# A state-space scan followed by a low-rank mixer: the list that orders every engine's work rewritten, the state's guard put on GpSimd, one step of the squares taken one word later

## The chip, the cores and the metric

The kernel runs on one core of a Trainium2 chip. Its five engines are TensorE (PE; PEld is its loading of weights), VectorE (DVE), ScalarE (ACT), GpSimd (POOL) and SyncE (SP), whose queue issues the DMAs. The metric is the time of one execution on the device, in microseconds (us); the median of several runs is compared.

## The reference

Two blocks follow each other. The first is a chunked scan with a state, the second mixes along the sequence by a product of rank 32 and then along the channels by a two-layer network.

```python
# x (4,8,768,32), a (4,8,768), B and C (4,8,768,16), fp32; chunks of 32
for c in range(nc):
    cum = np.cumsum(la, axis=-1)                # la: log a of this chunk
    L = np.exp(cum[:, :, :, None] - cum[:, :, None, :]) * causal
    M = np.einsum('bhin,bhjn->bhij', Cc, Bc) * L
    y_intra = np.einsum('bhij,bhjd->bhid', M, xc)
    y_inter = np.einsum('bhin,bhnd->bhid', Cc, state) * np.exp(cum)[:, :, :, None]
    y[:, :, sl] = y_intra + y_inter
    state = decay_full[:, :, None, None] * state + np.sum(Bx, axis=2)
# y as x (4, 768, 256); U (768,32), V (32,768), w_ch1 (256,1024), w_ch2 (1024,256)
u = x + (x.transpose(0, 2, 1) @ U @ V).transpose(0, 2, 1)
out = u + np.maximum(u @ w_ch1, 0.0) @ w_ch2
```

U, V, w_ch1 and w_ch2 are 64-bit floats in memory.

## The kernel before

There are four batches. The scan of a batch is cut along the sequence into three blocks of two 128-row tiles; a block is numbered k, twelve in all. The mixer of a batch works on three blocks j of 256 rows.

All work is written down in one list, the string of PLANS[1]. The function follow (L1070) takes its words one after the other and calls the step that each names; nothing is reordered afterwards, so the order of the words sets the order of each engine's queue, of SP's too. A word of the scan is a letter and a block, counted from batch 1: P-3 to P-1 are batch 0, P0 to P2 batch 1, P6 to P8 batch 3. The letters that the text below speaks of are:

- B, X, w, L: loads, issued by SP (L202). The first DMA of such a word is held until the last VectorE instruction written before the word has ended.
- c: a piece of the conversion of 64-bit words to fp32 (L409, VectorE and ScalarE), R: the refinement of a converted weight into three parts, near and low on ScalarE, far and both on VectorE (L447; a word is one half of it). Each part of such a step is called by a word of its own.
- P, D: B and C times their decays, on VectorE (D of batch 0 on POOL); T: their transposes; g: the products C with B; m, M: the causal mask on VectorE.
- s, u: the new state, its products and its update on VectorE; the copy Sm masked for each half of the heads (L654 on POOL in batch 0, L658 on ScalarE afterwards).
- n, i, j: the products within a chunk (L746), and with the state (L721), which are written in two words in batch 0: i, and j, the crossed half. y: the copies of the result, yT (L761, L766, L768, ScalarE). t: yT turned back into rows, O the same in batch 0.

A word of the mixer carries the batch as what it lags behind: U1.j.i and f1.j.i are batch 0, f0 batch 1, f-1 batch 2, f-2 batch 3. p is the product with U and its copy pT (L815), x the product with V, a the addition of it on VectorE. Blocks 0 and 1 of batch 0 use plain products (U, d1.0, d1.1) with the converted weights; all others use three products in the fp32r format with a split operand (S): f takes the first two terms, near and low, and a scaling on ScalarE (L858), e the third and the Relu, h the far and joined parts on VectorE, d the second layer in pieces, one a word.

From block 6 on the transposes of P's result go another way (squared, L543): VectorE transposes 32 by 32 squares, SP sends them to memory and fetches them back, turned, into T, and ScalarE makes the masked copy Cm from T (L558). The second T word of a block is the fetch and Cm.

The guard of the state concerns the two halves that write the same rows of a bank. The products of word j may only start when those of word i have ended. For this the first product of j waits for an instruction of another engine that had to come later anyhow: a mask, an update, a copy or an addition that was recorded between them (follows, L661). Where there is none, a one-column copy called settled is put on VectorE (apart, L666), which waits for the earlier products.

## Time and profile before

| what | us |
| --- | --- |
| runs of the kernel | 213.56, 214.67, 217.28 |
| median | 214.67 |
| profiled execution, its span | 216.2 |

The profiled execution is the one that all rows below are from. Its span, 216.2 us, lies between the second and the third run; it runs from the first to the last instruction that the profiler saw. In the rows, L177 stands for nearly all of VectorE's instructions, since a helper records them there; they are told apart by the tiles that they write and read. In the part that names who waited, "A <- B" says that A waited until B had ended.

### The profile page before, as it was taken

Reading aid. Unit: us, or ns where it says so; the run is one execution under the profiler, and the core shown is the slowest. Engines: PE = TensorE matmul, PEld = TensorE weight load, DVE = VectorE, ACT = ScalarE, POOL = GpSimd, SP = SyncE. Lnnn points to the kernel's source line nnn. Section 1 sums busy time; section 2 is a strip of 40 time slices with the busy share of each in tenths; the row PEclk is TensorE's granted clock in tenths of the full one; section 3 lists DMA queues with packets and bytes.
Section 4 is the critical chain, followed back from the end, with each engine's and each line's share of the span. In section 5 each row is a group of like instructions: output and inputs, shape, how many; then the busy total and the mean of one; then the engine's idle time right before and its main releaser. Section 6 shows DMA issues by size and latency. Waiting matters only on the chain.

```text
span 216.2 us, 7556 instructions
## 1 busy us (share of the span) xinstructions
PE 205.8 (95%) x3214; PEld 183.6 (85%) x3214; DVE 173.4 (80%) x363; ACT 121.0 (56%) x279; POOL 6.3 (3%) x22
## 2 busy tenths in 40 slices
PE   7988987999999999999999999899999999999994
PEld 4766755787889997998999998589998999999993
DVE  4498869988999999999899986759966398759841
ACT  3454646659968857186488451668612675444310
POOL 4121000000000000000000000000000000000000
PEclk9999997999999999999999999999999999999999
DMA  6998677996553379447666846544600000323344
GB/s 89 123 117 197 76 186 170 218 247 149 77 71 52 65 195 124 110 60 102 92 103 108 190 91 150 80 74 100 137 12 0 0 5 0 52 38 64 48 97 97
DMA packets 120177, 21.43 MB, mean 99 GB/s; under 512 B 110096, under 2 KB 118352, under 8 KB 120144
## 3 DMA queue, kind: packets, MB, share of 16 engines
q1 hardware_dynamic: 120144, 20.95, 53.3%
q8 instruction: 25, 0.41, 0.9%
q14 instruction: 8, 0.07, 0.1%
HBM read 14.39 MB, written 6.55 MB: 97 GB/s over the span
## 4 chain that ended last, share of the span: by engine, by line
PE 62%; DVE 22%; SPq 5%; ACT 4%; issue 3%; DMA 2%; POOL 0%; DVEq 0%; POOLq 0%; ACTq 0%
PE x L853 28%; PE z L853 21%; DVE words L177 7%; SPq L203 5%; DVE S L177 3%; DMA words<-in_moe_w_ch_dram 2%; DVE yT L177 2%; DVE w L177 2%; DVE M L177 2%; DVE BC L177 1%; PE x L139 1%; PE w L626 1%; PE x L591 1%; DVE u L177 1%; PE z L746 1%
## 5 line engine op out<-in xcount | busy, mean ns | idle before, releaser
L177 DVE SCALAR_TENSOR_TENSOR words<-words 128x512 fp32r<-128x512 f32 (+6 forms) x60 | 39.3, 668 | 2.6 <-ACT words L429 0.5
L853 PE MATMUL x<-words,w 128*128 128x256 f32 x288 | 38.5, 281 | 0.1
L853 PEld LDWEIGHTS x<-words,w 128*128 128x128 f32 x288 | 35.3, 189 | 1.8 <-issue 1.2
L853 PE MATMUL x<-u,w 128*128 128x256 f32 x240 | 34.6, 283 | 0.0
L853 PE MATMUL z<-u,w 128*128 128x256 f32 x240 | 33.0, 279 | 0.0
L858 ACT ACTIVATE x<-x 128x512 f32<-128x512 f32 (+1 forms) x27 | 15.5, 577 | 29.6 <-PE x L853 27.5
L853 PEld LDWEIGHTS x<-u,w 128*128 128x128 f32 x240 | 30.5, 188 | 0.6 <-ACT yT L766 0.3
L853 PEld LDWEIGHTS z<-u,w 128*128 128x128 f32 x240 | 30.0, 188 | 0.1
L858 ACT ACTIVATE z<-z 128x512 f32<-128x512 f32 (+1 forms) x24 | 13.6, 572 | 12.7 <-PE z L853 12.7
L853 PE MATMUL z<-words,w 128*128 128x256 f32 x144 | 19.9, 282 | 0.0
L853 PEld LDWEIGHTS z<-words,w 128*128 128x128 f32 x144 | 18.1, 189 | 0.9 <-issue 0.9
L177 DVE SCALAR_TENSOR_TENSOR words<-x,words 128x512 fp32r<-128x512 f32 x20 | 13.7, 683 | 5.4 <-ACT words L893 5.4
L177 DVE SCALAR_TENSOR_TENSOR words<-z,words 128x512 fp32r<-128x512 f32 x20 | 13.6, 682 | 2.3 <-ACT words L893 2.2
L893 ACT ACTIVATE words<-x 128x512 fp32r<-128x512 f32 x20 | 12.0, 598 | 3.6 <-PE x L853 3.6
L591 PE MATMUL x<-Cm,T 32*64 32x128 f32 x192 | 12.1, 310 | 1.6 <-DVE yT L177 1.2
L177 DVE TENSOR_TENSOR yT<-x,yT 128x384 f32<-128x384 f32 (+1 forms) x15 | 9.2, 614 | 5.5 <-PE x L853 2.7
L177 DVE SCALAR_TENSOR_TENSOR S<-S,kept,w 128x64 f32<-128x64 f32 x40 | 11.2, 279 | 2.3 <-PE w L626 0.6
L893 ACT ACTIVATE words<-z 128x512 fp32r<-128x512 f32 x20 | 11.8, 598 | 1.9 <-PE x L853 1.3
L658 ACT ACTIVATE Sm<-S,slot 128x128 f32<-128x128 f32 (+1 forms) x18 | 6.0, 386 | 9.9 <-DVE S L177 9.9
L591 PEld LDWEIGHTS x<-Cm,T 32*64 32x64 f32 x192 | 7.5, 131 | 4.1 <-DVE yT L177 1.5
L177 DVE TENSOR_TENSOR BC<-bc,F 128x512 f32<-128x512 f32 (+2 forms) x18 | 8.8, 517 | 2.6 <-ACT F L379 1.3
L591 PE MATMUL z<-Cm,T 32*64 32x128 f32 x192 | 10.5, 311 | 0.0
(154 smaller groups left out, 368.5 us busy)
## 6 DMA issues: line engine op xcount, KB each, us to landing
words<-in_moe_w_ch_dram SPq DMA_DIRECT2D x7, 512.0 KB, 5.3
squares<-w1f SPq DMA_DIRECT2D x52, 64.0 KB, 1.9
x<-in_x_dram SPq DMA_DIRECT2D x24, 128.0 KB, 4.0
out_dram<-o SPq DMA_DIRECT2D x32, 64.0 KB, 2.2
bc<-in_B_dram SPq DMA_DIRECT2D x24, 64.0 KB, 3.5
bc<-in_C_dram SPq DMA_DIRECT2D x12, 128.0 KB, 3.8
T<-squares SPq DMA_DIRECT2D x6, 256.0 KB, 3.9
ytok<-squares SPq DMA_DIRECT2D x6, 256.0 KB, 3.1
```

The source lines that it names most:

```text
L139: nc.tensor.matmul(out=t[:, :m * w].rearrange("p (m i) -> p m i", i=w), lhsT=ident, rhs=ident[:, None, :w].to_broadcast([P, m, w]), start= ...
L177: self.last = call(*args, **kwargs)
L203: op = nc.sync.dma_start(**kwargs)
L591: nc.tensor.matmul(out=g[r][cols, c], lhsT=s["T"][rows, 0, c, cols], rhs=s["Cm"][rows, :, :, ts(2 * c + p, Q)].rearrange("r v t i -> r v i ...
L626: nc.tensor.matmul(out=s["A"][p][ts(r, Q), v], lhsT=s["bd"][half, v, 2 * r:2 * r + 2].rearrange("p h n -> p (h n)"), rhs=x_sb[k][half, v, ...
L658: nc.scalar.activation(s["Sm"][:, sl, v], s["S"][:, sl, ts(v, D)], AF.Copy, scale=slot[:, v, None])
L746: product = nc.tensor.matmul(out=y[n][p][ts(v, Q), c], lhsT=x_sb[k][half, c, h], rhs=s["M"][half, h // 2, c, h % 2], start=fresh(k, n, p, ...
L853: nc.tensor.matmul(out=t, lhsT=lhsT, rhs=rhs, start=start, stop=True, skip_group_check=True)
L858: nc.scalar.activation(t, t, AF.Copy, scale=1.0 + EPS)
L893: nc.scalar.activation(gs[j, i][0], t, AF.Relu, scale=NEAR)
```

## The change

The list of PLANS[1] is written anew: the same words in another order, and one more T word for each of the blocks T3 to T8. That word is for the squares: two more yields stand between the fetch and the masked copy, so that Cm is recorded with the third T word instead of the second. The guard is no longer looked for: every j word, three in all, gets a settled copy, now on GpSimd, which waits for the products before it and for which the first product of j waits. The other lines of the diff (ASIDE, FARPOOL) are switches that stay off, and a buffer's allocation at whichever half comes first. VectorE then has two copies less, GpSimd three more; the totals of all other instructions are equal.

```diff
@@ PLANS[1], the part up to the first long product @@
-        'i-3 g-2 u-2 j-3 y-3 F2 g-1 i-2 B3 B4 B5 w2 w3 X3 w4 X4 m-2 M-2 w5 c0 c0 m-1 B6 O-3.0 c0 M-1 '
-        'w6 E-1.1 n-2 s-1 u-1 c2 v0 w7 c1 c2 j-2 F3 i-1 y-2 j-1 n-1 c1 y-1 P0 D0 c1 T0 c2 t-2 O-1.3 '
-        'P2 X5 T0 X6 w8 P1 D2 p1.0.4 p1.4.6 c3 c3 x1 a1.0 a1.1 T1 T2 T2 T1 g0 U1.0.0 c3 c4 c4 U1.0.1 '
+        'u-2 n-3 g-2 m-2 i-3 w2 j-3 B3 w0 w1 y-3 M-2 B5 c0 c0 F2 g-1 c0 m-1 M-1 B4 w3 i-2 n-2 '
+        'E-1.1 s-1 u-1 w6 c3 O-3.0 X3 v0 P0 j-2 y-2 c2 F3 i-1 n-1 c1 c1 c1 X4 w4 P2 t-2 D0 w8 '
+        'j-1 w5 y-1 p1.0.4 c2 O-1.3 w7 X5 T0 c2 T2 p1.4.6 P1 D1 T0 B6 x1 a1.0 T2 L4 T1 c3 a1.1 '
+        'T1 g0 c3 U1.0.0 c7 c4 c4 U1.0.1 m0 U1.1.0 M0 c4 R2 R0 g1 m1 c7 s0 u0 U1.1.1 M1 c5 c5 s1 '
...
@@ squared @@
         fetch(s["T"].rearrange("p i c t -> p (i c) t"), d, sent)
+        yield
+        yield
         for i in range(2):
             nc.scalar.activation(s["Cm"][:, i], s["T"][:, 1], AF.Copy, scale=slot[:, i, None])
         yield
@@ update, mask, added, ytokening: their calls of follows go @@
-    def follows(op, turn):
-
-        if turn == behind["turn"]:
-            behind.setdefault("part", op)
-
-    def apart(copy):
-
-        behind["part"] = op = copy(out=settled, in_=slot[:, :1])
+    def apart():
+
+        op = nc.gpsimd.tensor_copy(out=settled, in_=slot[:, :1])
         for product in behind["first"]:
             tc.add_manual_dep(op.ins, product.ins.name, mybir.DependencyInfo(
                 mybir.DependencyClass.Sync, mybir.DependencyReason.DATA))
+        return op
@@ inter @@
-        if part and "part" not in behind:
-            apart(vector.tensor_copy)
-        after = behind.pop("part", None)
-        if part == 0:
-            after = None
-            behind["turn"] += 1
-        else:
+        after = None
+        if part:
+            after = apart()
             behind["first"] = []
```

What the rewritten list moves shows best in the queues. In the rows that follow, each gives the line, the operation, the tile written and the tiles read with their numbers in the program, and the shape.

The first place is the start, ahead of U1.0.0. SP's queue between U's words and the fourth load of w_ch1, before: words_325 is w0 and w1, bc_442, bc_446 and bc_450 are B3, B4 and B5 (three DMAs each, the C one shown), words_454 is w2.

```order
L203 DMA words_325<-in_moe_w_ch1_dram 128x2x256 x2
...
L203 DMA bc_442<-in_C_dram 128x8x32
...
L203 DMA bc_446<-in_C_dram 128x8x32
...
L203 DMA bc_450<-in_C_dram 128x8x32
...
L203 DMA words_454<-in_moe_w_ch1_dram 128x2x512
```

And now: words_402 is w2, bc_411 is B3, words_415 is w0 and w1, bc_422 is B5, bc_461 is B4.

```order
L207 DMA words_402<-in_moe_w_ch1_dram 128x2x512
...
L207 DMA bc_411<-in_C_dram 128x8x32
...
L207 DMA words_415<-in_moe_w_ch1_dram 128x2x256 x2
...
L207 DMA bc_422<-in_C_dram 128x8x32
...
L207 DMA bc_461<-in_C_dram 128x8x32
```

w2 has moved from the end of this set to its head, and B4 from the middle to the end.

VectorE's queue at the same place before, from P2 and P1 (BC) over D2 (bd) and the conversion c3 of w2 (words_706) to the four additions a1.0 and a1.1 (yT):

```order
L177 TENSOR_TENSOR BC_673<-bc_450,F_149 128x512
L177 TENSOR_TENSOR BC_688<-bc_446,F_149 128x512
L177 TENSOR_TENSOR bd_690<-bc_450,FD_150 128x256
L177 TENSOR_SCALAR words_706<-words_454 128x512 x2
L177 TENSOR_TENSOR yT_158<-x_712,yT_158 128x384
L177 TENSOR_TENSOR yT_158<-z_714,yT_158 128x384
L177 TENSOR_TENSOR yT_158<-x_713,yT_158 128x384
L177 TENSOR_TENSOR yT_158<-z_715,yT_158 128x384
```

And now, where BC_701 is P1 and bd_703 is D1:

```order
L181 TENSOR_TENSOR BC_701<-bc_461,F_149 128x512
L181 TENSOR_TENSOR bd_703<-bc_461,FD_150 128x256
L181 TENSOR_TENSOR yT_158<-x_714,yT_158 128x384
L181 TENSOR_TENSOR yT_158<-z_716,yT_158 128x384
L181 TENSOR_TENSOR yT_158<-x_715,yT_158 128x384
L181 TENSOR_TENSOR yT_158<-z_717,yT_158 128x384
L181 SCALAR_TENSOR_TENSOR words_533<-words_532,words_533 128x512
```

P2 stands far ahead now, the conversion of w2 has begun before this row of work and ends behind it, and P1 has come right before the additions.

GpSimd's queue in batch 0 before, the copies Sm of the state and the last D words:

```order
L488 TENSOR_TENSOR bd_289<-bc_91,FD_150 128x256
L654 TENSOR_TENSOR Sm_337<-S_336,slot_145 128x256
L654 TENSOR_TENSOR Sm_396<-S_395,slot_145 128x256
L488 TENSOR_TENSOR bd_268<-bc_95,FD_150 128x128
L654 TENSOR_TENSOR Sm_547<-S_546,slot_145 128x192
```

And now:

```order
L668 TENSOR_TENSOR Sm_288<-S_287,slot_145 128x256
L505 TENSOR_TENSOR bd_294<-bc_95,FD_150 128x128
L668 TENSOR_TENSOR Sm_333<-S_332,slot_145 128x256
L677 COPY settled_155<-slot_145 128x1
L505 TENSOR_TENSOR bd_294<-bc_95,FD_150 128x128
L668 TENSOR_TENSOR Sm_525<-S_524,slot_145 128x192
L677 COPY settled_155<-slot_145 128x1 x2
```

Three settled copies have come, the first behind the second Sm, the other two behind the third.

The second place is the middle, where VectorE refines the weights for the first fp32r products. Before, the last rows up to the refinement R1, whose two rows are those of words_1234 and the w12_79 behind it; the pair before it is R0:

```order
L177 SCALAR_TENSOR_TENSOR S_1172<-S_1172,kept_151,w_1093 128x64
L177 TENSOR_TENSOR words_1179<-w1f_80,w10_77 128x512
L177 SCALAR_TENSOR_TENSOR w12_79<-words_1179,w10_77 128x2x256
L177 TENSOR_TENSOR BC_1188<-bc_482,F_149 128x512
L177 TENSOR_TENSOR u1_1191<-yT_158,u0_1190 128x512
L177 SCALAR_TENSOR_TENSOR u2_1192<-u0_1190,u1_1191 128x512
L177 TENSOR_TENSOR words_1234<-w1f_80,w10_77 128x512
L177 SCALAR_TENSOR_TENSOR w12_79<-words_1234,w10_77 128x2x256
```

And now, where R1 is the pair of words_1240, and pairs that read o belong to the second layer's weights, R5:

```order
L181 TENSOR_TENSOR u1_1197<-yT_158,u0_1196 128x512
L181 SCALAR_TENSOR_TENSOR u2_1198<-u0_1196,u1_1197 128x512
L181 TENSOR_TENSOR words_1220<-w1f_80,w10_77 128x512
L181 SCALAR_TENSOR_TENSOR w12_79<-words_1220,w10_77 128x2x256
L181 TENSOR_TENSOR words_1224<-o_928,w20_81 128x512
L181 SCALAR_TENSOR_TENSOR w22_83<-words_1224,w20_81 128x512
L181 TENSOR_TENSOR words_1236<-w1f_80,w10_77 128x512
L181 SCALAR_TENSOR_TENSOR w12_79<-words_1236,w10_77 128x2x256
L181 TENSOR_TENSOR words_1240<-w1f_80,w10_77 128x512
L181 SCALAR_TENSOR_TENSOR w12_79<-words_1240,w10_77 128x2x256
```

R0, R5 and R3 now stand as three pairs ahead of R1; before, R0 alone did, and R2 and R5 came behind.

The third place is ScalarE's queue where batch 3's scan meets batch 2's mixer. Before, from the copies Sm over y6 (yT_2453) to the near part of batch 2's first block (u0):

```order
L658 ACTIVATE Sm_2399<-S_2398,slot_145 128x3x32 x2
L768 COPY yT_2453<-x_2405 128x2x64
L768 COPY yT_2453<-z_2407 128x2x64
L766 COPY yT_2453<-x_2406 64x2x64 x2
L766 COPY yT_2453<-z_2408 64x2x64 x2
L815 COPY pT_2461<-w_2462 128x128
L558 ACTIVATE Cm_2279<-T_2278,slot_145 128x256 x2
L847 ACTIVATE u0_2564<-yT_1758 128x512
```

And now:

```order
L672 ACTIVATE Sm_2382<-S_2381,slot_145 128x4x32 x2
L819 COPY pT_2453<-w_2454 128x128
L772 COPY yT_2480<-x_2417 128x2x64
L772 COPY yT_2480<-z_2419 128x2x64
L770 COPY yT_2480<-x_2418 64x2x64 x2
L770 COPY yT_2480<-z_2420 64x2x64 x2
L577 ACTIVATE Cm_2301<-T_2300,slot_145 128x256 x2
L850 ACTIVATE u0_2600<-yT_1722 128x512
```

The copy pT has moved from behind the copies of y6 to ahead of them.

More of the change, by code (lines that the diff above doesn't have):

```diff
@@ L17 @@
 PLAIN = 2
+ASIDE = 99
+FARPOOL = False
 SQUARED = 6
@@ L439, in to_fp32 @@
             w2f[n] = dst
+        if aside:
+            nc.gpsimd.tensor_tensor(out=dst, in0=wide(rest), in1=wide(power.bitcast(FP32)),
+                                    op=ALU.mult)
+            yield
+            return
         vector.scalar_tensor_tensor(
@@ L467 @@
     UU = const.tile([P, NC, 2, RK], FP32)
-    behind = {"turn": 0, "first": []}
+    behind = {"first": []}
     yT, ytok = {}, {}
@@ L737, in intra @@
         y = channels(k)
-        behind.pop("part", None)
-        behind["turn"] += 1
         for n in range(2):
@@ L789, in ytokening @@
             copy = nc.scalar.copy if b < 2 else vector.tensor_copy
-            behind.setdefault("part", copy(out=out, in_=t))
+            copy(out=out, in_=t)
         yield
@@ L824, in mixed @@
             hold["h"] = h
-            hold["turn"] = behind["turn"]
         def added(k):
@@ L830, in added @@
                 u = uT[:, n, ts(k, VS)]
-                follows(vector.tensor_tensor(
-                    out=u, in0=hold["h"][2 * n + k][:, :VS], in1=u, op=ALU.add), hold["turn"])
+                vector.tensor_tensor(
+                    out=u, in0=hold["h"][2 * n + k][:, :VS], in1=u, op=ALU.add)
         def block(j):
@@ L864, in plain @@
         def plain(j, i):
-            if i % 2 == 0:
+            if (j, i // 2) not in gT:
                 gT[j, i // 2] = words(FP32)
```

28 lines of the change are left out of this document (16 added, 12 removed), and 57 rows, old and new, of the table PLANS.

## The prediction

> **What bounds the kernel now.** I read the profile's page first (the busy times), then the busy time of each engine by stage, then, where an engine waits, its timeline.
>
> ```profile
> span 216.2 us, 7556 instructions
> PE 205.8 (95%) x3214; PEld 183.6 (85%) x3214; DVE 173.4 (80%) x363; ACT 121.0 (56%) x279; POOL 6.3 (3%) x22
> 17.00:36.00 19.00, 15.54 (x371) 11.45 (x372) 15.12 (x41) 11.57 (x29) 1.48 (x3) 0.97 0.75 149
> 36.00:66.00 30.00, 29.69 (x534) 24.30 (x533) 27.58 (x63) 21.70 (x51) 0.00 (x0) 0.96 0.74 154
> 66.00:98.00 32.00, 31.98 (x437) 28.74 (x438) 31.17 (x61) 21.32 (x45) 0.00 (x0) 1.00 0.56 103
> 98.00:132.00 34.00, 33.87 (x623) 32.16 (x613) 29.98 (x61) 20.06 (x52) 0.00 (x0) 1.00 0.65 114
> 132.00:145.00 13.00, 12.30 (x423) 9.59 (x412) 10.05 (x24) 7.21 (x24) 0.00 (x0) 1.00 0.50 95
> ```
>
> The five stage rows give from:to, length, then busy time of PE, PEld, DVE, ACT, POOL, then the granted clock, the DMA share and GB/s. From 36 us on TensorE is the bound: 29.69 of 30, 31.98 of 32, 33.87 of 34. The change reorders work and takes no matmul away, so all that a better order can win is PE's idle time: 3.46 us in 17 to 36 (19.00 - 15.54), about 0.5 in 36 to 132, 0.7 in 132 to 145. What a worse order can lose is not bounded so: VectorE stands at 31.17 of 32 between 66 and 98, so PE's rest there hangs on VectorE being in time. The start is another regime; there DMA and VectorE decide when the first long product (U1.0.0) may begin:
>
> ```profile
> 19.18 0.63 DVE L177 TENSOR_SCALAR words<-words 128x384 int32<-128x384 int32 x2 [0.87 <-DMA words<-in_moe_U_dram]
> 21.92 0.75 DVE L177 TENSOR_TENSOR M<-z,causal 128x256 int32<-128x256 int32 x2
> ...
> 30.10 1.29 DVE L177 TENSOR_TENSOR BC<-bc,F 128x512 f32<-128x512 f32 x2 [1.29 <-DMA bc<-in_B_dram]
> 31.31 0.42 DVE L177 TENSOR_TENSOR bd<-bc,FD 128x256 f32<-128x256 f32 x1
> 32.83 0.76 DVE L177 TENSOR_SCALAR words<-words 128x512 int32<-128x512 int32 x2 [1.10 <-DMA words<-in_moe_w_ch_dram]
> 33.51 0.55 DVE L177 TENSOR_TENSOR yT<-x,yT 128x384 f32<-128x384 f32 x1
> ...
> 34.91 0.55 DVE L177 TENSOR_TENSOR yT<-z,yT 128x384 f32<-128x384 f32 x1
> 30.39 0.49 PE L822 MATMUL z<-V,pT 32*128 32x384 f32 x2
> 35.46 3.40 PE L853 MATMUL x<-yT,w1f 128*128 128x256 f32 x8
> 38.70 1.67 PE L853 MATMUL z<-yT,w1f 128*128 128x256 f32 x7
> ```
>
> Start, length, and in brackets the engine's idle time and what ended it. VectorE waits for the B and C of block 2 until 30.10 (its words P2 and P1 follow, then D2), then for the third load of w_ch1 (w2) until 32.83; only then come the four additions a1.0 and a1.1 (33.51 to 35.46), and U1.0.0 starts with their end, 35.46. The products x1 that they add were ready at 30.88 (30.39 + 0.49). U1.0.0 itself took 3.40 where the next eight took about 1.7: the clock was at half.
>
> **The change, part by part.** The sum is made against the profiled span, 216.2, which is 0.7% above the median 214.67; I carry the difference over to the median.
>
> *Loads, and the start (T0, the start of U1.0.0).* Between U's words (19.18) and w2 (32.83) SP brings w0, w1, three B and C sets and w2. Afterwards w2 goes first, and the set that P1 needs (block 1, B4) last, held until the mask words of block 1. The conversion of w2 no longer stands ahead of a1.0, but P1 now waits for the end of the same set. Early end: B4 is held only until M-1 (its last row here ends near 22.67), so it can be in before PE's chain is ready; that chain gets the guards below. Ready is then x1: 30.88 plus up to 1.5 for the guards (below) is 32.4; the four additions take 1.95 (35.46 - 33.51) and T0 is 34.3. Late end: the same bytes at the same rate, so B4 lands where w2 did, 32.83; then P1 (0.64, half of 1.29), D1 0.42, 1.95: T0 = 35.8. The row nearest is the second, since all rows of this set end by that rate; but the hold speaks for the first. I take 35.5 (0.0), and keep -1.2 and +0.4.
>
> *Guards.* Two copies on VectorE go, three come on GpSimd.
>
> ```profile
> L177 DVE COPY settled<-slot x2: 145/150/155, 16.8 to 25.1; 128x1 f32<-128x1 f32 x2
> PEld z L721 <- DVE settled L177: 1.0, 2, 0.5
> 0.31 0.10 POOL L1107 MEMSET const-float32-0.0<- 128x1 f32 x1 [0.31 <-issue]
> 2.69 0.24 POOL L315 COPY onward<-low 128x64 f32<-128x64 f32 x1
> 23.57 0.51 POOL L654 TENSOR_TENSOR Sm<-S,slot 128x192 f32<-128x192 f32 x1 [5.59 <-DVE S L177]
> ```
>
> One column on GpSimd is bounded by 0.10 (nothing read) and 0.24 (64 columns); I take 0.15, the same as on VectorE. So the copy costs nothing by itself; the waiting of PE (0.5 each) comes back three times instead of two, and a guard that stands behind a Sm on GpSimd (0.51), as two of the three do, can be later by that much. Together 0.5 (one more wait) to 1.5 (that and two Sm) on PE's chain of the start, which is part of the term above and is covered as long as B4 or VectorE is later. Without that cover it is the early end's T0. The Trainium skill, page "GPSIMD Engine Reference", section 3.1, speaks against the move: it puts two software dispatch hops on GpSimd against one on VectorE, and measures 1.96 times VectorE's time for an addition. By that ratio a guard would take 0.29, an estimate, and three of them 0.4 more than I count; no GpSimd copy of one column is in this trace, and the 64-column row is already shorter.
>
> *Third T word.* The masked copy Cm waits less at the head of ScalarE's queue:
>
> ```profile
> ACT Cm L558 <- DMA T<-squares: 3.4, 2, 3.0
> 117.00:126.00 9.00, 9.00 (x123) 8.78 (x129) 8.78 (x14) 4.59 (x10) 0.00 (x0) 1.00 0.74 167
> ```
>
> 3.4 us of waiting go, but PE was busy 9.00 of 9.00 around the longer of the two. What hides it is the matmul queue (d words); gain 0, and at most 0.2 if a Relu behind it was just late.
>
> *The middle, 36 to 70.* Two refinements, R5 and R3, now stand ahead of R1, whose low part f1.2.1 needs, and f1.2.1 comes right behind f1.2.0.
>
> ```profile
> 35.45:65.73 30.28, 29.97 (x537) 24.53 (x533) 27.86 (x63) 21.99 (x51) 0.00 (x0) 0.95 0.73 151
> 65.73 0.69 DVE L177 TENSOR_TENSOR words<-w1f,w 128x512 f32<-128x512 f32 x1
> 66.45 0.69 DVE L177 SCALAR_TENSOR_TENSOR w<-words,w 128x512 fp32r<-128x512 f32 x1
> 67.94 0.63 ACT L458 ACTIVATE w<-words 128x512 fp32r<-128x512 f32 x1
> 65.29 1.09 PE L776 MATMUL w<-ident,yT 128*128 128x128 f32 x8
> 66.22 1.89 PE L853 MATMUL z<-words,o 128*128 128x256 f32 x8
> 67.95 1.89 PE L853 MATMUL x<-words,o 128*128 128x256 f32 x8
> 69.49 1.74 PE L853 MATMUL x<-u,w 128*128 128x256 f32 x12
> ```
>
> VectorE: 27.86 of work between T0 and R1's first row (65.73), plus four rows of 0.69 (R5, R3) is 30.6; plus R1's first 0.69 and the low part on ScalarE 0.63 is 31.9; plus VectorE's waits, 2.4 before (30.28 - 27.86), of which some vanish as it has more to do: 0.5 to 2.4. So f1.2.1's operand is there at T0 + 32.4 to 34.3. PE: f1.2.0 stood at T0 + 34.0 (69.49 - 35.46); the transposes t0 (0.93, from 65.29 to 66.22) and one piece of d1.0 (1.73, from 66.22 to 67.95) move behind, and f1.2.0 itself, 8 products of the 12 in 1.74, adds 1.1: T0 + 32.4. PE then waits 0 to 1.9; I take 0.7, near the low end, since a busier VectorE waits less. From this the wait at U1.1.3 goes, partly:
>
> ```profile
> 49.76 1.99 PE L853 MATMUL z<-yT,w1f 128*128 128x256 f32 x8 [0.31 <-ACT yT L766]
> ```
>
> -0.3. Middle: +0.4, ends -0.3 and +1.6. What of it is won back later is little: PE has no idle time to give until 132.
>
> *Batch 3's entry, 132 to 145.* The copy pT is now ahead of the copies y6 on ScalarE:
>
> ```profile
> 133.34 1.53 PE L810 MATMUL w<-ytok,UU 128*64 128x128 f32 x24
> 136.39 0.27 ACT L815 COPY pT<-w 128x128 f32<-128x128 f32 x1
> 136.71 0.59 PE L822 MATMUL x<-V,pT 32*128 32x384 f32 x2 [0.60 <-ACT pT L815]
> ```
>
> The project p-1 ended at 134.87, its copy ran at 136.39, PE waited 0.60. That wait can go; but the products x-1 take banks that y6 has to empty, and y6 waits for the last transposes of the buffer yT that it writes, which now come later (behind the last d0.2 words instead of d0.1). Both ends lie within PE's 0.7 of idle time and twice as much lost: -0.7 to +1.0, I take 0. In the tail the order of the last d and h words differs, with each third part ready before its piece by the rows' lengths: 0.
>
> Sum: 0.0 + 0 + 0 + 0.4 + 0 = +0.4: a span of 216.6, and on the median 215.1.
>
> **The rivals.**
> A. *VectorE falls behind and stays behind.* Same start as my middle term, but at its upper end, and repeated at the next blocks: with 31.17 of 32 busy in 66 to 98 it can't catch up, so each refinement moved ahead of its due time is paid by PE. Per R pair 1.4; it becomes slower by over 2% (4.3 us) when three such pairs are paid for in full, say at f1.2.1, at f0.2 (whose blocks now come before f0.1) and in batch 3: 214.7 + 4.3 = 219. For it: the high DVE share. Against it: the instruction totals are equal and R5 and R3 were due anyway. 0.12. A milder form, 1 to 3 us, counts with my forecast.
> B. *B4 late.* T0 = 35.8 plus what the reordered SP queue adds; if B5 and B4 queue behind w2's 0.5 MB, a set of B and C later than I think is the 2.7 that w2 took (32.83 - 30.10), of which half would show: 216.5. 0.15, within 2%.
> C. *No half clock at the start.*
>
> ```profile
> 28.10:31.52 3.42, 2.49 (x34) 1.63 (x34) 2.13 (x5) 1.67 (x5) 0.00 (x0) 1.00 0.70 154
> 31.52:34.93 3.41, 2.24 (x35) 1.51 (x40) 2.31 (x7) 2.04 (x5) 0.00 (x0) 1.00 0.95 253
> 34.93:38.34 3.41, 3.41 (x31) 2.54 (x13) 3.38 (x9) 1.67 (x5) 0.00 (x0) 0.50 0.60 165
> ```
>
> The clock was 0.50 for just the 3.41 us behind a stretch in which PE was busy 2.24 of 3.41; the stretch before, with 2.49, was followed by 1.00. If PE's wait of 1.2 near 33 shrinks, U1.0.0 takes 1.7 instead of 3.40: -1.7, and with T0 1.0 earlier, near its early end, -2.7: 212.0. But VectorE then must keep up in the middle, where I have it late already, so most of it is lost there. 0.18, faster by 1 to 3 us, still within 2%. The Trainium skill, "TensorE: Matmul & The Clock Gate", Part 1: The HAM clock gate, gives a free-running window of about 3.4 us and half clock after an idle one; the length agrees with 34.93 to 38.34, but the window ahead wasn't idle, so the trace's own bound (2.24 against 2.49) goes here.
> D. *The change ends nothing.* All moved waits were covered and no new one appears: 214.7 within the spread of the runs (213.56 to 217.28). 0.20.
>
> **How the numbers follow.** My forecast 0.35, A 0.12, B 0.15, C 0.18, D 0.20. The time is the likeliest case's, 215.1. The low end takes in most of C (212.0), the high end B and the milder A: 215.1 + 1.2 (middle at its end) + 1.0 (batch 3) + 0.4 (T0) = 217.7, and a little of A itself: 218.2. Some 0.08 lies above and 0.1 below. Two per cent, 4.3 us, is about what a measurement of this kernel can tell from no change. Faster by that: only C with batch 3's gain and an unseen one more, 0.05. Slower by that: A, 0.12. Within: 0.83.
>
> **What would show it.** First U1.0.0's start (35.5, from 34.3 to 35.8), and what VectorE waits for before the additions: a DMA of bc, no longer words of w_ch. The granted clock just behind. The settled copies on POOL at 0.10 to 0.24, and PE's waits for them, some 0.5 each. No wait of Cm for the squares above 1 us. A wait of PE at f1.2.1, near 68, for an ACT copy of w: 0 to 1.9. VectorE's share from 66 to 98 at 0.97 or more. PE's idle time from 132 to 145 about 0.7. I am wrong if PE idles over 1 us anywhere between 40 and 130, if the start differs by over 1 us, or if the tail behind 195 shows PE waiting.

## The result, and the profile after

The changed kernel took 217.53 us (median of 20 runs, 215.93 to 220.88) beside 215.92 for the kernel before on the same chip (20 runs, 213.56 to 220.28). The ratio is 1.0095 (95%: 1.0065 to 1.0124); it leaves disturbed executions out, so it isn't the quotient of the two medians. The kernel became slower by some 2.0 us. A second measurement (e1 below) gave 1.0203 (1.0148 to 1.0257), or 4.4 us. The forecast was +0.4, on the right side but short by 1.6 to 4.0. On its base of 214.67 the two ratios make 216.7, inside its range of 212.0 to 218.2, and 219.0, above it. The profiled execution lasted 220.07 us, longer than most of its runs; where a reading rests on it, a second profile of the same kernel (e1) is named beside it.

First the page of the changed kernel, its totals and its instruction queue, then busy time by stage. The columns are those shown in the prediction (PE, PEld, DVE, ACT, POOL, granted clock, DMA share, GB/s).

```profile
span 218.4 us, 7574 instructions
PE 204.8 (94%) x3214; PEld 182.3 (83%) x3214; DVE 174.0 (80%) x361; ACT 121.8 (56%) x279; POOL 7.0 (3%) x25
q8 instruction: 25, 0.41, 0.8%
```

```profile
17.00:36.00 19.00, 15.49 (x374) 11.08 (x375) 15.05 (x40) 11.27 (x29) 1.89 (x6) 1.00 0.82 163
36.00:66.00 30.00, 27.36 (x524) 21.75 (x523) 27.78 (x62) 22.23 (x54) 0.00 (x0) 1.00 0.78 149
66.00:98.00 32.00, 32.00 (x350) 28.94 (x350) 30.06 (x56) 20.38 (x40) 0.00 (x0) 1.00 0.49 94
98.00:132.00 34.00, 33.76 (x695) 31.68 (x694) 29.08 (x60) 20.45 (x52) 0.00 (x0) 1.00 0.68 117
132.00:145.00 13.00, 11.74 (x330) 9.44 (x310) 11.21 (x28) 6.17 (x21) 0.00 (x0) 1.00 0.45 90
```

PE's idle time has risen at two places: from 0.31 to 2.64 us in 36 to 66 (30.00 less 29.69 and 27.36), and from 0.70 to 1.26 in 132 to 145. Elsewhere it stands as it stood. The count of matmuls is the same, 3214, and PE's busy time 204.8 against 205.8.

**The place in the middle** is one single gap. The timeline of PE there (start, length, and in brackets the idle time and what ended it), and the two stretches around it:

```profile
46.83 0.45 PE L750 MATMUL x<-M,x 64*32 64x64 f32 x32
47.10 0.44 PE L750 MATMUL z<-M,x 64*32 64x64 f32 x14
50.02 0.38 PE L750 MATMUL z<-M,x 64*32 64x64 f32 x18 [2.48 <-issue]
```

```profile
46.00:48.00 2.00, 1.54 (x73) 0.95 (x72) 1.93 (x5) 1.55 (x5) 0.00 (x0) 1.00 1.17 232
48.00:50.00 2.00, 0.00 (x0) 0.00 (x0) 1.97 (x4) 0.00 (x0) 0.00 (x0) 1.00 0.47 45
```

PE stops in the middle of n0, after 14 of 32 equal products that read the same two tiles as the other 18, so late data is no likely cause. The bracket says "issue": the engine waited for nothing that the profile shows. ScalarE, which waits for PE's results, does nothing either from 48 to 50. What arrives in that gap shows in the DMA view, here of two stretches, 37 to 47.2 and 47.2 to 49:

```profile
q1 hardware_dynamic: 4578, 2.54, 90.8%
...
words<-in_moe_w_ch_dram SPq DMA_DIRECT2D x4, 512.0 KB, 6.6
...
q1 hardware_dynamic: 1893, 0.18, 91.3%
q8 instruction: 1, 0.02, 4.2%
```

The queue q8 carries a program in pieces of 16 KB (25 of them, 0.41 MB, over the execution). That it is PE's is read from the DMA records: in all fourteen profiles the last piece comes when PE has begun 6302 to 6314 of its weight loads and products. In 37 to 47.2 not one came, while loads kept the 16 DMA engines 91% busy; the next began at 47.33, ended at 48.55, and PE went on 1.5 us later. The loads in front are four of 512 KB, as SP's queue has them:

```profile
38.03 2.38 SPq L207 DMA_DIRECT2D words<-in_moe_w_ch_dram  x4
40.51 3.57 SPq L207 DMA_DIRECT2D x<-in_x_dram  x2
44.17 3.28 SPq L207 DMA_DIRECT2D bc<-in_B_dram  x1
```

That is w4, w8, w5 and w7 in one go, and X5 behind them. In the list before, w5 stands 14 words ahead of w7, and w7 some 20 ahead of w8. From the DMA records of the instruction queue, for the piece that PE needs behind its 1729th instruction (weight loads and products counted):

| kernel | piece on its way, us | PE stands in n0, us |
|---|---|---|
| before | 42.42 to 44.15 | 0 |
| before, second profile (e7) | 43.40 to 44.34 | 0 |
| changed | 47.33 to 48.55 | 2.5 |
| changed, second profile (e1) | 46.28 to 47.65 | 1.9 |

The same place recurs. In all five profiles with a stand in n0 (these two, and e5, e6 and e10 below) PE stops behind that same 1729th instruction, and goes on 1.3 to 1.6 us after the piece has landed.

**The place in batch 3** is n7. The waits view of 130 to 150, the timeline of PE and that of VectorE:

```profile
PE x L750 <- DVE yT L181: 0.9, 1, 0.9
```

```profile
139.93 0.42 PE L750 MATMUL x<-M,x 64*32 64x64 f32 x23 [0.88 <-DVE yT L181]
```

```profile
138.43 1.00 DVE L181 STREAM_TRANSPOSE w1f<-yT 128x256 f32<-128x256 f32 x2 [1.11 <-ACT yT L770]
139.36 0.52 DVE L181 TENSOR_TENSOR yT<-x,yT 128x384 f32<-128x384 f32 x1
```

The wait for pT (0.60 before) is gone. In its place n7 waits 0.88 for a bank that the additions a-1.0 and a-1.1 must read first, and these stand behind the transposes t6 on VectorE, which in turn waited 1.11 for ScalarE's copies of y6. In the list, the first word t6 has moved from behind y8 to ahead of a-1.0.

### The profile page after: what moved, and what is told of

Its sections match the earlier page's. It is cut to its first block, busy times and chain, and to the rows that moved or that the text cites. A ratio compares the mean times of both kernels' runs of the same rounds, so it can differ in the third digit from the quotient of the medians.

```text
span 218.4 us, 7574 instructions
## 1 busy us (share of the span) xinstructions
PE 204.8 (94%) x3214; PEld 182.3 (83%) x3214; DVE 174.0 (80%) x361; ACT 121.8 (56%) x279; POOL 7.0 (3%) x25
## 4 chain that ended last, share of the span: by engine, by line
PE 80%; issue 4%; DVE 4%; SPq 4%; DMA 3%; ACT 2%; POOL 1%; POOLq 0%; DVEq 0%; ACTq 0%
PE x L856 36%; PE z L856 29%; SPq L207 3%; DMA bc<-in_B_dram 3%; PE w L814 2%; PE x L609 2%; PE z L750 2%; PE x L727 2%; PE x L750 2%; PE w L641 1%; ACT yT L770 1%; DVE yT L181 1%; PE x L143 1%; PE x L522 1%; DVE BC L181 1%
## 5 line engine op out<-in xcount | busy, mean ns | idle before, releaser
L856 PE MATMUL x<-words,w 128*128 128x256 f32 x288 | 39.4, 283 | 0.0
L856 PE MATMUL z<-u,w 128*128 128x256 f32 x240 | 33.9, 283 | 0.3 <-ACT yT L770 0.3
L856 PE MATMUL x<-u,w 128*128 128x256 f32 x240 | 34.1, 283 | 0.0
L181 DVE TENSOR_TENSOR M<-x,causal 128x256 int32<-128x256 int32 x24 | 9.0, 418 | 3.7 <-PE z L609 3.7
L609 PE MATMUL x<-Cm,T 32*64 32x128 f32 x192 | 10.6, 307 | 0.3 <-ACT Cm L577 0.2
L750 PE MATMUL z<-M,x 64*32 64x64 f32 x384 | 8.1, 225 | 2.5 <-issue 2.5
```

Of the source, the lines that this page charges most:

```text
L181: self.last = call(*args, **kwargs)
L609: nc.tensor.matmul(out=g[r][cols, c], lhsT=s["T"][rows, 0, c, cols], rhs=s["Cm"][rows, :, :, ts(2 * c + p, Q)].rearrange("r v t i -> r v i ...
L750: product = nc.tensor.matmul(out=y[n][p][ts(v, Q), c], lhsT=x_sb[k][half, c, h], rhs=s["M"][half, h // 2, c, h % 2], start=fresh(k, n, p, ...
L856: nc.tensor.matmul(out=t, lhsT=lhsT, rhs=rhs, start=start, stop=True, skip_group_check=True)
```

## The experiments

All times are compared with the kernel before on the same chip in the same stretch of runs, where its median was 214.22 to 214.66. The edits are to the list of words, where two lists meet at a word by which both have done the same work. The results, with the stands of PE that each profile shows:

| run | what it is | ratio, 95% | piece of program starts | stand in n0 | half clock from 45 to 210 us |
|---|---|---|---|---|---|
| e1 | changed, again | 1.0203 [1.0148, 1.0257] | 46.28 | 1.9 | 49.56 to 52.98 |
| e2 | guards and third T word alone | 1.0041 [0.9996, 1.0085] | 40.56 | 0 | none |
| e4 | old list to g2, then new | 1.0251 [1.0196, 1.0306] | 40.76 | 0 | none |
| e5 | w8 and X5 much later | 1.0231 [1.0185, 1.0278] | 44.71 | 0.5 | none |
| e6 | new list to 124 us, then old | 1.0115 [1.0063, 1.0166] | 47.02 | 2.4 | 49.73 to 53.14 |
| e7 | before, again | 1.0006 [0.9971, 1.0041] | 43.40 | 0 | none |
| e8 | e5, and R1 first | 1.0241 [1.0206, 1.0275] | 43.75 | 0 | 56.89 and 142.22 |
| e9 | before, with w6 to w8 bunched | 1.0045 [1.0009, 1.0082] | 43.60 | 0 | none |
| e10 | w8 behind X5 | 1.0117 [1.0085, 1.0149] | 44.50 | 1.1 | 139.60 |
| e11 | w7 and w8 behind X5 | 1.0097 [1.0062, 1.0132] | 44.20 | 0 | 139.32 |
| e12 | e11 to 124 us, then old | 1.0029 [0.9996, 1.0062] | 43.55 | 0 | none |
| e13 | e11 to 47 us, then old | 1.0065 [1.0029, 1.0102] | 43.34 | 0 | none |

One more list, e3 (the new one up to g1, then the old one), has no time: its engines would wait for each other in a circle. e13 below cuts at a later word.

### e1: the changed kernel a second time

No edit. Its place here is to tell what recurs from what one execution shows.

> The changed kernel once more, unaltered. In its profile PE stood 2.5 us in the middle of n0, at 47.5, with all operands long there, and a 16 KB fetch on the instruction queue ran from 47.33 to 48.55; the fetch before had been at 35.79, PE had run through 408 instructions since. Theory 1 (code fetch late behind the loads, a property of this order): the stand comes again at n0 or near it, 1 to 3 us, and the ratio to the kernel before is 1.006 to 1.013. Theory 2 (a single event of that profile): no stand there, PE waits at f1.2.1 instead, about 1.8, for R1's low part, and the ratio is the same, since VectorE then ends last.

Measured: 218.46 us, ratio 1.0203. The stand in n0 recurs, 1.9 us, with a late piece of program again. What differs is behind it. The windows of the clock in this run:

```profile
46.15:49.56 3.41, 1.46 (x93) 1.03 (x74) 3.34 (x6) 1.37 (x5) 0.00 (x0) 1.00 0.83 115
49.56:52.98 3.42, 3.42 (x37) 2.58 (x32) 2.92 (x10) 2.29 (x7) 0.00 (x0) 0.50 0.71 85
```

PE was busy 1.46 of 3.41 us in the window with the stand, and the next ran at half clock. In the first profile of the changed kernel the same stand brought no half clock; by the same 3.41 us steps it lay across two windows there, with PE busy 1.93 and 2.41. So the stand costs its own length and, in some executions, up to 1.7 more (half of 3.4); this may be why the two measurements of the ratio differ, but no run isolates it.

### e2: the guards and the third T word alone

The kernel before with the changed code: three settled copies on GpSimd, and each third T word right behind its second, so that no other word moves.

```diff
-'h1.2.0 P5 d1.1 e1.2.2 f1.2.3 e1.2.1 p0 T3 d1.2 e1.2.3 T4 T5 L6 h1.2.2 h1.2.1 R7 d1.1 x0 '
+'h1.2.0 P5 d1.1 e1.2.2 f1.2.3 e1.2.1 p0 T3 T3 d1.2 e1.2.3 T4 T4 T5 L6 h1.2.2 h1.2.1 R7 d1.1 x0 '
...
-        behind["part"] = op = copy(out=settled, in_=slot[:, :1])
+        op = nc.gpsimd.tensor_copy(out=settled, in_=slot[:, :1])
```

> The list of before, with the changed code: three settled copies on GpSimd, and the third T word right behind the second, so that Cm keeps its place. Theory 'the list alone costs': ratio 0.998 to 1.002. Rival 'the guards cost': PE stands 0.7 at j-3 and 1.6 at j-2 for settled in the changed kernel against 0.5 and 0.5 before; if that is the guard itself and not what is queued ahead of it, U1.0.0 starts 0.5 to 1.2 us later than at 35.46 and the ratio is 1.003 to 1.006.

Measured: 1.0041 [0.9996, 1.0085]. In its profile PE does each product from U1.0.0 to 150 us no later than in e7, the kernel before: 0.0 to 0.2 us earlier, and up to 0.4 near 132. The guards and the T word thus cost nothing that shows in the trace; a ratio of up to 0.85% isn't excluded by the times. With 2.03% for the whole change on the same chip (e1), most of the loss there is the new order's.

### e4: the old start, the new rest

The old list up to g2 (some 47 us), then what is left in the changed order. It was to say which half of the list the loss is in.

```diff
-'n0 y0 c6 c6 s1 c5 g2 c7 u1 R2 m2 c7 U1.1.3 M2 c8 c8 c7 U1.0.2 L4 i1 n1 y1 c6 R1 R0 c8 s2 '
+'n0 y0 c6 c6 s1 c5 g2 L4 c7 R2 R0 c7 U1.0.2 u1 c7 m2 L6 U1.0.3 R5 R3 M2 U1.1.3 c8 c6 c8 s2 '
...
```

> The other half: the list of before up to the word g2 (PE at 49), then the words that are left in the order of the changed kernel. Theory 1 (the start carries the loss): ratio 0.998 to 1.004, of which up to 0.8 us from 126 to 147. Rival (VectorE behind in the middle): PE waits 1 us or more at f1.2.1 and the ratio is 1.005 to 1.012.

Measured: 219.4 us, ratio 1.0251, more than the whole change. The profile gives the reason, a wait that neither parent has:

```profile
53.78 1.99 PE L856 MATMUL z<-yT,w1f 128*128 128x256 f32 x8 [2.52 <-DVE M L181]
```

U1.1.3 waits for the mask M2. At the seam that mask stands on VectorE behind the conversion c7, whose pieces wait 1.15 and 0.96 us for ScalarE; in the new list some of c7 was done ahead of g2. So e4 isn't a clean half, and its ratio says nothing of either. What it does show is that with the old order of loads there is no stand in n0.

### e5: w8 and X5 out of the bunch

The changed list, with the words w8 and X5 moved behind M1.

```diff
-'X4 w4 P2 t-2 D0 w8 j-1 w5 y-1 p1.0.4 c2 O-1.3 w7 X5 T0 c2 T2 p1.4.6 P1 D1 T0 B6 x1 a1.0 '
-'T2 L4 T1 c3 a1.1 T1 g0 c3 U1.0.0 c7 c4 c4 U1.0.1 m0 U1.1.0 M0 c4 R2 R0 g1 m1 c7 s0 u0 U1.1.1 M1 c5 c5 s1 '
+'X4 w4 P2 t-2 D0 j-1 w5 y-1 p1.0.4 c2 O-1.3 w7 T0 c2 T2 p1.4.6 P1 D1 T0 B6 x1 a1.0 '
+'T2 L4 T1 c3 a1.1 T1 g0 c3 U1.0.0 c7 c4 c4 U1.0.1 m0 U1.1.0 M0 c4 R2 R0 g1 m1 c7 s0 u0 U1.1.1 M1 X5 w8 c5 c5 s1 '
```

> The changed list with two loads moved: w8 and X5 stand behind M1 (VectorE at 44) instead of ahead of j-1 and T0, so that SP no longer queues w4, w8, w5, w7 and X5 within 38 to 42. Theory 'the code fetch waits behind the queued loads': the fetch that started at 47.33 and 46.28 starts some 1.5 to 3 us earlier (0.5 MB at the 0.33 to 0.4 MB per us of that stretch, and X5), the stand of 1.9 to 2.5 in n0 goes or falls below 0.8, and the time is 1.5 to 3 us less than the changed kernel's in the same call's terms: ratio 1.005 to 1.012 where the changed kernel had 1.0203. Rival 'PE's stand is not the bound, VectorE is': the stand goes, PE waits 1 us or more at f1.2.1 instead, ratio 1.015 to 1.022.

Measured: 219.57 us, ratio 1.0231, the number that the rival gave. By the profile it isn't the rival's reason: the piece of program starts at 44.71 instead of 47.33, and the stand shrinks from 2.5 to 0.5. But both loads now miss their own users:

```profile
55.56 0.32 PE L641 MATMUL w<-x,bd 64*32 64x64 f32 x8 [1.14 <-DMA x<-in_x_dram]
...
57.06 0.76 DVE L181 TENSOR_SCALAR words<-words 128x512 int32<-128x512 int32 x2 [2.73 <-DMA words<-in_moe_w_ch_dram]
```

One wait was traded for others, PE 1.14 us for X5 and VectorE 2.73 for w8; and at f1.2.1 PE waits 0.56 for R1's low part. The time misses the theory; the trace of the stand bears it out.

### e6: the old order behind 124 us

The changed list up to the words d0.1 near 124 us, then the old one.

```diff
-'d0.2 d0.2 h0.1.1 d0.2 d0.1 h0.2.1 d0.2 d0.2 d0.1 d0.2 h0.1.2 h0.1.0 d0.1 d0.1 d0.2 d0.1 '
+'d0.2 d0.2 h0.1.1 d0.2 d0.1 h0.2.1 d0.2 d0.2 d0.1 D8 u6 h0.1.2 h0.1.0 d0.1 d0.1 d0.2 '
...
```

> The changed list up to the d0.1 word at about 124, then the words that are left in the order of before. The changed kernel lost another 1 us of PE time between 124 and 147 against the list of before. Theory 'that stretch is a part of its own': ratio 1.013 to 1.018, some 1 us less than the 1.0203 of the changed kernel. Rival 'it is only how the same waits are spread': ratio 1.018 to 1.024.

Measured: 216.67 us, ratio 1.0115 [1.0063, 1.0166]. Beside e1 (1.0203) and the first measurement (1.0095) this doesn't decide by itself whether the late part costs. The stand in n0 is there (2.4), the one in n7 is not.

### e7: the kernel before a second time

No edit.

> The kernel before, unaltered, for a profile without the half clock at U1.0.0 and of the usual rate behind 150. Ratio 1.00. If 0.50 comes in only some executions, U1.0.0 takes 1.7 here and the span is 211 to 213.5; theory 'its PE gap of 1.2 near 33 always brings the half clock' has 3.4 at U1.0.0 again.

Measured: 1.0006 [0.9971, 1.0041], as it must be. Its use is its profile: U1.0.0 starts at 34.16 and runs at the full clock (its first eight products in 1.99), where the profile that the prediction read had 35.46 and half clock. The half clock of the start is here at 16.88 to 23.71. So neither the late start nor the half clock at U1.0.0 is a property of the kernel before; both are of one execution. That execution was a long one: time and span differ by 1.7 us in the profiles that have both (220.07 and 218.4 in the changed kernel), so its span of 216.2 stands for some 217.9, an estimate, above all three times of the table ahead of the prediction.

### e8: e5 with R1 ahead

The same as e5, and the second halves of R5 and R3 put behind R1, to undo the prediction's middle term.

```diff
-'c9 u2 i1 n1 d1.0 X6 d1.1 c8 c9 n2 i2 P4 S1.2 y1 y2 t1 R0 R5 L5 R1 R3 R1 d1.0 d1.0 d1.1 '
+'c9 u2 i1 n1 d1.0 X6 d1.1 c8 c9 n2 i2 P4 S1.2 y1 y2 t1 R0 L5 R1 R1 R3 R5 d1.0 d1.0 d1.1 '
```

> As with w8 and X5 moved, and the second halves of R5 and R3 put behind R1's, where R3 and R5 stood relative to it before. Theory 'VectorE ahead of R1 binds once the fetch is in time': R1's low part is there 2.8 us earlier, the wait at f1.2.1 goes, and the time is 0.5 to 1.8 us below that with the loads moved alone. Rival 'it is hidden': equal within 0.4 us.

Measured: 219.22 us, ratio 1.0241, the same as e5 within the intervals. The late X5 and w8 cost as in e5 (PE waits twice 1.0 us for X5), so R1's place can't be read from the time alone. In the trace the 0.56 that e5 waits at f1.2.1 is gone; no run here shows a gain in time.

### e9: the bunch put into the kernel before

The reverse test: the kernel before, with w6, w7 and w8 right behind w5.

```diff
-'i-3 g-2 u-2 j-3 y-3 F2 g-1 i-2 B3 B4 B5 w2 w3 X3 w4 X4 m-2 M-2 w5 c0 c0 m-1 B6 O-3.0 c0 M-1 '
-'w6 E-1.1 n-2 s-1 u-1 c2 v0 w7 c1 c2 j-2 F3 i-1 y-2 j-1 n-1 c1 y-1 P0 D0 c1 T0 c2 t-2 O-1.3 '
-'P2 X5 T0 X6 w8 P1 D2 p1.0.4 p1.4.6 c3 c3 x1 a1.0 a1.1 T1 T2 T2 T1 g0 U1.0.0 c3 c4 c4 U1.0.1 '
+'i-3 g-2 u-2 j-3 y-3 F2 g-1 i-2 B3 B4 B5 w2 w3 X3 w4 X4 m-2 M-2 w5 w6 w7 w8 c0 c0 m-1 B6 O-3.0 c0 M-1 '
+'E-1.1 n-2 s-1 u-1 c2 v0 c1 c2 j-2 F3 i-1 y-2 j-1 n-1 c1 y-1 P0 D0 c1 T0 c2 t-2 O-1.3 '
+'P2 X5 T0 X6 P1 D2 p1.0.4 p1.4.6 c3 c3 x1 a1.0 a1.1 T1 T2 T2 T1 g0 U1.0.0 c3 c4 c4 U1.0.1 '
```

> The kernel before with its loads w6, w7 and w8 right behind w5, so that SP has 2 MB of weights queued at once, as the changed list has; all else as before. PE reaches its 1470th instruction at 39 to 41 and the code fetch of that place came at 42.4 and 43.4. Theory 'a code fetch waits behind the loads queued ahead of it': the fetch that falls into the bunch starts 1.5 to 4 us later than PE's need for it grows, PE stands 0.5 to 2.5 with all operands there, and the ratio is 1.004 to 1.015. Rival 'the stand belongs to the new order of PE's own words': no stand, ratio 0.997 to 1.003.

Measured: 216.04 us, ratio 1.0045 [1.0009, 1.0082], no stand, the piece of program at 43.60 as in e7 (43.40). A miss. The bunch was issued at 35.3 to 38.3 here and had landed by 45.3, so the piece still came in time: a bunch does no such harm wherever it stands. That it must lie just ahead of the piece fits this, but was not tested by a second place. The reverse of the effect was not produced, and the 0.45% is not accounted for.

### e10 and e11: one load, then two, behind X5

The bunch taken apart with as small a move as the users of the loads allow: w8 alone behind X5, and w7 and w8 behind X5.

```diff
-'X4 w4 P2 t-2 D0 w8 j-1 w5 y-1 p1.0.4 c2 O-1.3 w7 X5 T0 c2 T2 p1.4.6 P1 D1 T0 B6 x1 a1.0 '
+'X4 w4 P2 t-2 D0 j-1 w5 y-1 p1.0.4 c2 O-1.3 w7 X5 T0 c2 T2 p1.4.6 P1 D1 T0 w8 B6 x1 a1.0 '
```

```diff
-'X4 w4 P2 t-2 D0 w8 j-1 w5 y-1 p1.0.4 c2 O-1.3 w7 X5 T0 c2 T2 p1.4.6 P1 D1 T0 B6 x1 a1.0 '
+'X4 w4 P2 t-2 D0 j-1 w5 y-1 p1.0.4 c2 O-1.3 X5 T0 c2 T2 p1.4.6 P1 D1 T0 w7 w8 B6 x1 a1.0 '
```

> The changed list with w8 alone moved, behind X5 and ahead of B6, which still lets it land by 50 where 55 is needed, and X5 by 49. Ahead of the code fetch stand w4, w5, w7 and X5 then, 0.5 MB or about 1.4 us less: theory 'the fetch waits behind the loads': it starts at 45 to 46 instead of 46.3 to 47.3, the stand in n0 is 0.5 to 1.2 instead of 1.9 to 2.5, nothing else waits, and PE's lag against the list of before falls from 4.6 to 3.2 to 3.8 us. Rival: stand and lag as they were.

> The same with w7 and w8 behind X5. Theory 'the fetch waits behind the loads': fetch at 44 to 45, stand 0 to 0.6, lag 1.8 to 3.0 us, ratio 1.006 to 1.014, 2 us or more below the changed kernel. Rival 'VectorE binds in any case from 50 to 70': the stand goes, waits of the same sum come at U1.0.3, s2 or f1.2.1, and the ratio stays at 1.018 to 1.024.

Measured: with one load moved the piece starts at 44.50 and PE stands 1.1; with two it starts at 44.20 and PE doesn't stand. SP's queue and PE in e11:

```profile
37.48 1.04 SPq L207 DMA_DIRECT2D words<-in_moe_w_ch_dram  x2
38.62 1.18 SPq L207 DMA_DIRECT2D x<-in_x_dram  x2
39.90 4.46 SPq L207 DMA_DIRECT2D words<-in_moe_w_ch_dram  x2
```

```profile
46.43 0.45 PE L750 MATMUL x<-M,x 64*32 64x64 f32 x32
46.70 0.72 PE L750 MATMUL z<-M,x 64*32 64x64 f32 x32
```

All 32 products of z run through in 0.72 where the changed kernel stopped after 14. Nothing but the place of two loads differs, and they are no operand of n0. But the ratios, 1.0117 and 1.0097, lie only 0.9% and 1.1% below e1's, less than the 1.2% that 2.5 us make, and not below the first measurement's 1.0095: a loss was left. Both profiles show it at n7, with a half clock behind it:

```profile
135.91:139.32 3.41, 2.43 (x113) 1.49 (x113) 3.30 (x7) 2.48 (x8) 0.00 (x0) 1.00 0.49 76
139.32:142.73 3.41, 3.41 (x41) 3.03 (x38) 3.31 (x11) 1.14 (x5) 0.00 (x0) 0.50 0.67 107
```

### e12: both repaired

e11, and behind 124 us the old order, by the same seam as e6.

> The changed list with w7 and w8 behind X5 and, from the d0.1 word at about 124 on, the words that are left in the order of before. With the two loads alone the ratio was 1.0097 and PE's lag against the list of before 1.4 at 122 and 2.3 to 2.7 from 131 to 145. Theory 'the new order from 124 to 147 costs by itself' (PE stands 1.1 in n7 until the additions a-1.1, behind t6): the lag stays near 1.4 behind 122, ratio 1.003 to 1.007. Rival 'no part of its own': 1.008 to 1.012.

Measured: 215.39 us, ratio 1.0029 [0.9996, 1.0062]. There is no stand in n0 and none in n7; the old wait for pT is back in its place, as the waits view of 130 to 150 and PE's timeline show, and the window ahead of 137.41 has PE busy 2.80 of 3.41, with the full clock behind it:

```profile
PE x L826 <- ACT pT L819: 0.6, 1, 0.6
```

```profile
135.08 0.59 PE L826 MATMUL x<-V,pT 32*128 32x384 f32 x2 [0.61 <-ACT pT L819]
```

```profile
134.00:137.41 3.41, 2.80 (x99) 1.52 (x82) 2.80 (x7) 2.11 (x7) 0.00 (x0) 1.00 0.49 75
```

Each repair also shows as a difference of times. e6 less e12, which differ in the place of w7 and w8 alone: 0.0115 - 0.0029 = 0.0086, plus or minus 0.0061 (both intervals taken as independent), 1.8 us for the stand in n0. e11 less e12, which differ in the order behind 124 us alone: 0.0068 plus or minus 0.0048, 1.5 us. These pairs ran on different chips, each against the kernel before on its own. Against the whole change the price of one repair depends on which measurement is taken: e1 less e11 is 0.0106 plus or minus 0.0065, the first measurement less e11 nil. Both repairs together show against either: 0.0174 plus or minus 0.0064 below e1, 0.0066 plus or minus 0.0044 below the first.

### e13: the repaired start alone

e11 up to y0 (47 us), then the old order.

```diff
-'U1.0.2 i0 u1 c7 n0 g2 y0 c5 c6 m2 c6 L6 U1.1.2 U1.0.3 R5 D2 R3 M2 U1.1.3 c8 c6 c8 s2 c9 '
+'U1.0.2 i0 u1 c7 n0 g2 y0 X6 D2 U1.1.2 c6 c6 c5 m2 U1.1.3 M2 c8 c8 i1 n1 y1 c6 R1 c8 s2 '
...
```

> The changed list with w7 and w8 behind X5 up to the word y0 (PE at 47), then all words that are left in the order of before. Theory 'the code fetch was what the start lost; the rest of the loss lies in the middle and behind 124': no stand in n0, lag 0 to 0.7 behind 60, ratio 0.998 to 1.004. Rival 'the start costs besides the fetch' (guards, the order of the loads): ratio 1.005 to 1.010.

Measured: 1.0065 [1.0029, 1.0102], more than e12, though it holds less of the change. PE's timeline shows a wait of the seam's own:

```profile
57.87 0.30 PE L750 MATMUL z<-M,x 64*32 64x64 f32 x3 [0.89 <-issue]
```

PE stands 0.89 in n2, again in the middle of equal products and again for "issue", while a later piece of program is on its way from 55.13 to 56.43; it stops behind its 2241st instruction, 512 further than in n0, and goes on 1.4 us after the piece has landed. X6, which the seam brings forward, has its loads issued at 52.37, just ahead; that these are the cause was not tested. U1.1.3 waits 0.6 for a conversion besides. The run doesn't price the start, then, but it shows the stand at a second piece of the program.

## Why the prediction came out as it did

**The sign was right, the size and the cause were not.** The sum had +0.4 for R1; what was measured is 2.0 to 4.4, from two things of which one had no term and the other was put at zero. That the sign came out, and the first time within the range, is luck: the wait that was to make the +0.4 did not come. Nor do the chances fit each other: 0.12 for a loss of over 4.3 us, which is above 219.0, and 0.08 for all that is above 218.2.

**Loads, the step that failed.** The prediction followed the moved loads to what waits for their data (the additions, P1, D2) and to the DMA rate, and gave the start a term of 0.0. For the start itself that holds: U1.0.0 began at 35.20 against a forecast of 35.5, and in the nine profiles with the new start at 33.96 to 35.20, beside 34.03 to 35.46 in the five with the old one. VectorE waits for a DMA of bc, as forecast, but for the set of block 2 (B5, at P2, the row at 30.08); P1, at 32.49, followed without a wait, near the 32.83 that the forecast had for B4. The timeline of VectorE ahead of U1.0.0, and its waits from 17 to 36:

```profile
30.08 0.69 DVE L181 TENSOR_TENSOR BC<-bc,F 128x512 f32<-128x512 f32 x1 [1.06 <-DMA bc<-in_B_dram]
...
32.49 0.68 DVE L181 TENSOR_TENSOR BC<-bc,F 128x512 f32<-128x512 f32 x1
...
34.82 0.55 DVE L181 TENSOR_TENSOR yT<-z,yT 128x384 f32<-128x384 f32 x1
```

```profile
DVE BC L181 <- DMA bc<-in_B_dram: 2.4, 2, 1.3
```

What it left out is that PE's own program comes by DMA beside the loads. With four loads of 512 KB issued within 2.4 us ahead of it, the next 16 KB of program landed at 48.55, 1.0 us after PE had run out (47.54). The prediction's own list of what would refute it, "PE idles over 1 us anywhere between 40 and 130", is what happened. The row was on the page of before, where the instruction queue has its 25 packets, but no time of PE was put down to it there because none was lost. Shown: that the stand goes when two loads that PE doesn't read are moved (e11), shrinks when one is (e10), and recurs with the old end (e6), each time behind the same instruction. Not shown: when the piece is asked for, since the trace has only its transfer, and so how much of the delay is waiting behind other packets and how much a late request.

**Batch 3's entry.** The prediction had named this place with both of its ends: "the products x-1 take banks that y6 has to empty", -0.7 to +1.0, and took 0. The wait for pT went as forecast (-0.60), and the loss came at the neighbouring bank: n7 waits 0.88 for the additions behind t6, and t6 waits for y6's copies. By e11 less e12 the order behind 124 costs 1.5 us (0.4 to 2.5), in the middle beyond the +1.0 of the upper end, which the interval still takes in. The wait alone isn't that much, 0.88 less the 0.60 that went; but the 0.88 recurs in all seven profiles with that order, and in three of them (e8, e10, e11) a window of half clock follows, which costs 1.7; in none of the seven with the old order there does one. So the term was mis-sized: it counted the stand and not the clock. The 0.28 and 1.7 in three of seven executions make some 1.0 on average, an estimate; what else of that order is in the 1.5 was not tested.

**The middle.** The forecast had PE wait 0.7 at f1.2.1 for R1's low part, and -0.3 at U1.1.3. PE's and ScalarE's timelines at f1.2.0 and f1.2.1:

```profile
68.86 1.27 PE L856 MATMUL x<-u,w 128*128 128x256 f32 x8
69.97 1.08 PE L856 MATMUL z<-u,w 128*128 128x256 f32 x8
```

```profile
68.67 0.63 ACT L475 ACTIVATE w<-words 128x512 fp32r<-128x512 f32 x1 [0.70 <-DVE words L181]
```

No wait: the low part was done at 69.30, f1.2.1 began at 69.97. PE was late itself, by the stand in n0, but e11 and e12 have no stand and no such wait either. Only e5, where VectorE had lost 2.73 us to w8, has it (0.56). So the mechanism exists, but VectorE wasn't late enough for it: the +0.4 that the forecast rested on didn't come, and the lower end (0) of that wait was right. The 0.31 at U1.1.3 went, as forecast.

**The guards.** Forecast 0.15 each, 0 in the sum. The tile's own row, and PE's wait for it:

```profile
L677 POOL COPY settled<-slot x3: 183/183/375, 17.2 to 26.8; 128x1 f32<-128x1 f32 x3
```

```profile
PEld z L727 <- POOL settled L677: 2.4, 3, 1.6
```

183 ns against the 150 of VectorE, and PE waits 2.4 us in all instead of 1.0. That is 1.4 more, within the 0.5 to 1.5 that was put on PE's chain at the start, and it is covered, as the prediction had it: e2, which has the guards and nothing else, starts U1.0.0 at 34.03, where e7 has 34.16. The Trainium skill ("GPSIMD Engine Reference", section 3.1) has 1.96 times VectorE's time for an addition; for this one column the ratio is 183/150 = 1.22.

**The third T word.** The waits on Cm in the whole execution are now these:

```profile
PEld x L609 <- ACT Cm L577: 0.4, 1, 0.4
...
PE x L609 <- ACT Cm L577: 0.2, 1, 0.2
```

ScalarE no longer waits 3.4 us for the squares, and PE was at 9.00 of 9.00 there before: 0 gained, as forecast.

**The rivals.** A (VectorE falls behind) is wrong: VectorE's share from 66 to 98 is 30.06 of 32, or 0.94, less than before; the prediction's signs had 0.97 or more. B (B4 late) is wrong by U1.0.0's start. C (no half clock at the start) had its sign in the profile after, U1.0.0 at full clock, and gave nothing, since e7 has it too. D is refuted by the interval. The share of the tail that the prediction put at 0 stays there: PE has no idle time behind 145.

**What stays open.** e12 leaves 0.3% (0 to 0.6), which nothing in its profile is put down to. It holds the guards and the third T word, and e2, which has these alone, measured 0.4% (0 to 0.85): they may be the rest, though e2's trace shows no loss. The parts add up to 0.29 + 0.86 + 0.68 = 1.83% (1.1 to 2.5: it is e6 plus e11 less e12), which fits the second measurement of the change (2.03%) better than the first (0.95%, up to 1.24); neither is excluded. No version beat the kernel before.

## What to carry to other kernels

Moving a load moves more than its user: PE's program comes by DMA too, in small pieces, and a bunch of large loads ahead of one stopped the engine in the middle of instructions whose operands are all there. When a profile shows a gap ended by "issue" inside a run of equal matmuls, look at the instruction queue in the DMA view of that stretch, and space the loads ahead of it. And before a term rests on where the half clock falls, take a second profile of the same kernel, since the window's place changed from one execution to the next.
